# Attention, Fourier mixing and a feed-forward part on one core: other steps for three folds, and another order of ScalarE's copies and exponentials

## The chip, the cores and the metric

The kernel runs on one core of one Trainium2 chip, in one launch. The metric is the device time of one execution in microseconds (us). A core has TensorE (PE in the profile), VectorE (DVE), ScalarE (ACT), GpSimd (POOL) and a queue for data transfers (SP). Each works through its own instructions in order and waits for the others by semaphores.

## The reference

For each of 4 images (batch entries) of 768 tokens, attention with 8 heads of 64, where a token sees the first 4 tokens (the sinks) and the last 128; then a Fourier transform over tokens and over channels, of which the real part is added; then layer norm and a feed-forward part of 512 to 2048 to 512 channels.

```python
scores = scale * np.matmul(q, k.transpose(0, 1, 3, 2))
keep = is_sink | in_window
scores = np.where(keep, scores, -1000000000.0)
a = np.exp(scores - np.max(scores, axis=-1, keepdims=True))
a = a / (np.sum(a, axis=-1, keepdims=True) + 1e-09)
x = np.matmul(a, v)                       # heads side by side: (4, 768, 512)
u = x + np.real(np.fft.fft(np.fft.fft(x, axis=1), axis=2))
un = (u - mean(u)) / np.sqrt(var(u) + 1e-06)
out = u + np.maximum(un @ w_ch1, 0.0) @ w_ch2
```

## The kernel before

**Attention.** An image has 6 blocks of 128 queries, 24 in all. A block has 4 steps, one for each pair of heads, so there are 96 steps and a few more to drain. In a step each engine issues a short list of operations, most of them for a pair of some steps ago (`STEP_LAG`, `BLOCK_AT`). For a pair of heads, TensorE computes scores (L700, L702) into PSUM tiles s, of which there are two: the matmul of a pair waits until VectorE has read the pair before the last. VectorE's `merge` (L708) puts the older keys' part into place, and `soft1` (L720, twice) adds the mask and takes the negative maximum. "Pair 0" to "pair 3" below are the merges and soft1 of one block. ScalarE's `expo` (L726, two instructions) takes the exponentials and their sums. TensorE transposes the result (pt, L751), ScalarE copies it (`copy_p`: pta, L758), GpSimd masks it into ptl and pta (`newer_p`, `older_p`: L767, L775), and TensorE multiplies with the values (xt, L789). The sinks' weights go another way: GpSimd packs them (`sink_p`: sk, L737, L738), TensorE transposes them into a free part of the s tile of pair 1, two blocks later (L809), and ScalarE copies them from there (`copy_sink`: skt, L814); the merge of that pair waits for the copy. `copy_x` (xs, L794), `turn_x` (x, L801, L803) and `store_x` (L819, VectorE) bring a finished block into u, the image in token order.

**Fourier part.** When an image's fourth block is stored, `fourier` enters the steps of its transform into an event table, counted from that step. First come three folds j = 0, 1, 2, each beginning 4 steps after the one before. A fold adds and subtracts block j and block j + 3 (`fold_n`, even and odd, L351), folds the channels (`fold_m`, L358 and L361), and splits the result into a rounded part gh (`fold_hi`, ScalarE, L364) and a remainder gl (`fold_lo`, VectorE, L367). In the first three images the even half runs on VectorE and the odd half on GpSimd. The row of token 0 is handled beside that: `put_row` (L380), `mid_sum` (L371), and `mid_row`, a cast into sph (L375) and a remainder for one row (L377), both on VectorE. Seven steps after the third fold began, matmuls with cosine and sine tables read gh, gl and sph (za, zr, zb, L394; then L421, L442), VectorE forms sums (d, L447, L448), and GpSimd adds them to u (L458, L459); images 1 and 3 are then stored to DRAM by SP (ud, L461).

**Order.** Three things set it. `SCHEDULE` has, for each phase (steps before and from 36) and each of the 4 steps of a block, the list of each engine; "V", "G", "A", "T" and digits in a list are where events of the table go. `F_N`, `F_M`, `F_S` and `ROW` are the steps of the folds. From step 97 on (`CUT`) the framework orders the instructions itself, which is where the fourth image's transform (its folds wholly on VectorE) and the conversion of the feed-forward weights (cv, L590 to L592) lie. The first three images' folds lie ahead of that.

**Feed-forward part.** From about 278 us on, TensorE multiplies with resident weights (h, L619; o, L1124) to the end.

Of the kernel before, what the change touches and what calls it, by code (L numbers as in the profile page):

```python
# [25 lines left out]
NHALF = NB // 2  # L26
# [8 lines left out]
NR = 33  # L35
# [25 lines left out]
FILL_AT, FILL = (24, 36), 0  # L61
FOLD_AT, FOLD_LAST, FOLD_ENG = (0, 4, 8), (0, 4, 8), "VG"

F_N, F_M, F_S, ROW = (3, 3), (4, 5), (6, 7), (5, 8, 10)
EV_A = 0

SINK0_AT = 3, 3, "V"
# [16 lines left out]
    {  # L84
        "A": [
            ["copy_x", "copy_p", "copy_sink", "expo", "A", "sink_hi"],
            ["copy_x", "copy_sink", "expo", "sink_hi", "A", "copy_p"],
            ["copy_x", "copy_p", "copy_sink", "expo", "A", "sink_hi"],
            ["copy_x", "A", "copy_p", "copy_sink", "expo", "sink_hi"],
        ],  # L90
        "V": [
            ["inverse", "store_x", "sink_lo", "V", 3, 0, 1, 2, "merge", "soft1"],
# [17 lines left out]
    {  # L110
        "A": [
            ["copy_x", "copy_p", "A", "sink_hi", "copy_sink", "expo"],
            ["copy_x", "copy_sink", "A", "sink_hi", "copy_p", "expo"],
            ["copy_x", "copy_p", "copy_sink", "expo", "A", "sink_hi"],
            ["expo", "copy_x", "copy_p", "copy_sink", "A", "sink_hi"],
        ],
# [89 lines left out]
def kernel(  # L206
# [15 lines left out]
    V, A, G, T = nc.vector, nc.scalar, nc.gpsimd, nc.tensor  # L222

    def f32(ap):
        return ap.bitcast(F32)
# [44 lines left out]
    def run(general):  # L270
        tag = "g" if general else ""
        with ExitStack() as p1:
# [8 lines left out]
            def at(s, eng, fn):  # L281
                ev.setdefault((s, eng), []).append(fn)
# [26 lines left out]
            sph = fpool.tile([P, 384], F32R, name="sph")  # L309
# [22 lines left out]
            def fourier(b, at, ready):  # L332
# [5 lines left out]
                t_ = {}  # L338
# [9 lines left out]
                def fold_n(eng, j, odd):  # L348
                    t = fw.tile([P, DM], F32, tag=f"f{odd}", name=f"f{odd}_{b}_{j}", bufs=2 - odd)
                    t_["eo", j, odd] = t  # L350
                    eng.tensor_tensor(t, u[j], u[NHALF + j], op=ALU.subtract if odd else ALU.add)  # L351

                def fold_m(eng, j, odd):

                    g = t_["eo", j, 0]
                    if odd:
                        t = t_.pop(("eo", j, odd))
                        eng.tensor_tensor(g[:, 257:512], t[:, 1:256], t[:, 511:256:-1], op=ALU.subtract)  # L358
                        t_["g", j] = t_.pop(("eo", j, 0))
                    else:  # L360
                        eng.tensor_tensor(g[:, 1:256], g[:, 1:256], g[:, 511:256:-1], op=ALU.add)  # L361

                def fold_hi(j):
                    A.copy(gh[:, j], t_["g", j])  # L364

                def fold_lo(j):
                    V.tensor_tensor(gl[:, j], t_.pop(("g", j)), f32(gh[:, j]), op=ALU.subtract)  # L367
# [2 lines left out]
                    r = t_["x0"]  # L370
                    V.tensor_tensor(r[:, 1:256], r[:, 1:256], r[:, 511:256:-1], op=ALU.add)  # L371

                def mid_row():
                    t = t_["x0"]
                    V.tensor_copy(sph[:NR, :257], t[:, :257])  # L375
                    lo = sph[NR - 1:NR, :257]
                    V.tensor_tensor(lo, t[NR - 1:NR, :257], f32(lo), op=ALU.subtract)  # L377

# [84 lines left out]
                tail = b == B - 1 or general  # L463
                at(1, "S", load_row)
                for j in range(NHALF):
                    k = ready[j]
                    e0, e1 = FOLD_TAIL if tail else FOLD_ENG
                    eng = {"V": V, "G": G}
                    at(k + F_N[0], e0, lambda j=j: fold_n(eng[e0], j, 0))
                    at(k + F_N[1], e1, lambda j=j: fold_n(eng[e1], j, 1))  # L470
                    at(k + F_M[0], e0, lambda j=j: fold_m(eng[e0], j, 0))
                    at(k + F_M[1], e1, lambda j=j: fold_m(eng[e1], j, 1))
                    at(k + F_S[0], "A", lambda j=j: fold_hi(j))
                    at(k + F_S[1], "V", lambda j=j: fold_lo(j))
# [862 lines left out]
```

## Time and profile before

| | us |
|---|---|
| runs of the kernel | 786.68, 789.1, 787.84; median 787.84 |
| the profiled execution | 786.78 |
| its span, first to last instruction | 784.9 |
| busy: PE / DVE / ACT / POOL | 755.2 / 460.6 / 239.0 / 177.6 |

The span divides roughly so: attention with the transforms of the first three images to about 222 us, the fourth transform beside the first group of the feed-forward part to 278, the rest of the feed-forward part to the end. In rows of the profile, "L367" is line 367 of the kernel before, "gl<-f,gh" names the tile written and those read, the first number is the start, the second how long one (or a merged run of "x4") took, and square brackets tell the idle time of the engine ahead of it with what ended it. Busy times of PE include its pipelining, so a busy PE need not be at its peak.

### The profile page before, as it was taken

How to read it: one execution, taken by the hardware profiler on the slowest of the kernel's cores; microseconds unless marked ns; L12 is line 12 of the kernel's file. 1: busy time of each engine (PE TensorE's matmuls, PEld its weight loads, DVE VectorE, ACT ScalarE, POOL GpSimd, SP SyncE). 2: the span in 40 equal slices, each digit the busy share in tenths (PEclk: the TensorE clock that was granted, in tenths of full speed). 3: DMA queues.
4: the chain of work that ended last, by engine and by line, in shares of the span. 5: the costliest groups of instructions: out<-in, count | busy, mean ns of one | idle time of the engine just before them, and what ended most of it. 6: DMA issues, size and time to landing. Idle time of an engine off the chain costs nothing.

```text
span 784.9 us, 11953 instructions
## 1 busy us (share of the span) xinstructions
PE 755.2 (96%) x4379; PEld 615.8 (78%) x4379; DVE 460.6 (59%) x1354; ACT 239.0 (30%) x704; POOL 177.6 (23%) x283
## 2 busy tenths in 40 slices
PE   7999998988899999999999999999999999999996
PEld 5666876866778878899888888888888888888895
DVE  6788687999999589561356424662456425611211
ACT  4887765756633133221111111111111110110110
POOL 2566477476645255200000000000000000000000
PEclk9999999999999999999999999999999999999999
DMA  9853525433305366120100002000200001000100
GB/s 311 251 171 109 140 84 176 127 112 99 131 27 159 111 196 210 62 71 1 54 1 0 1 9 99 1 1 0 81 1 0 1 0 54 1 1 0 55 1 32
DMA packets 41812, 57.69 MB, mean 74 GB/s; under 512 B 2796, under 2 KB 27500, under 8 KB 41360
## 3 DMA queue, kind: packets, MB, share of 16 engines
q1 hardware_dynamic: 41456, 53.07, 21.7%
q0 software_dynamic: 288, 3.76, 1.2%
q8 instruction: 37, 0.61, 0.3%
q14 instruction: 31, 0.25, 0.1%
HBM read 47.37 MB, written 9.45 MB: 72 GB/s over the span
## 4 chain that ended last, share of the span: by engine, by line
PE 80%; DVE 13%; issue 2%; POOL 1%; ACT 1%; DMA 1%; SPq 0%; DVEq 0%; ACTq 0%; POOLq 0%
PE h L619 33%; PE o L1124 33%; PE xt L789 3%; PE s L702 3%; DVE sm L720 2%; PE pt L751 2%; DVE cv L591 1%; PE za L394 1%; DVE s L708 1%; DVE cv L590 1%; PE a L421 1%; DVE cv L592 1%; DVE f L351 1%; PE x L801 1%; DMA vt<-in_v_sink_dram 1%
## 5 line engine op out<-in xcount | busy, mean ns | idle before, releaser
L1124 PE MATMUL o<-w,h 128*128 128x512 f32 x876 | 216.5, 394 | 0.0
L1117 DVE SCALAR_TENSOR_TENSOR h<-h,h 128x512 fp32r<-128x512 f32 (+1 forms) x107 | 65.4, 611 | 247.7 <-ACT h L1112 247.5
L1124 PEld LDWEIGHTS o<-w,h 128*128 128x128 f32 x876 | 162.8, 188 | 35.5
L1112 ACT ACTIVATE h<-h 128x512 fp32r<-128x512 f32 (+1 forms) x107 | 57.2, 535 | 366.4 <-PE h L619 360.1
L619 PE MATMUL h<-un_slots,w 128*128 128x512 f32 (+1 forms) x576 | 124.7, 365 | 0.0
L619 PEld LDWEIGHTS h<-un_slots,w 128*128 128x128 f32 x576 | 99.6, 188 | 19.6
L619 PE MATMUL h<-un_last,w 128*128 128x512 f32 (+1 forms) x432 | 89.0, 355 | 0.0
L619 PEld LDWEIGHTS h<-un_last,w 128*128 128x128 f32 x432 | 72.7, 188 | 12.8
L726 ACT ACTIVATE sm<-sm,mx 128x132 f32<-128x132 f32 x192 | 75.8, 400 | 7.1 <-DVE mx L720 7.1
L1148 DVE STREAM_TRANSPOSE unf<-un 32x128 f32<-32x128 f32 x224 | 67.7, 302 | 3.2
L702 PE MATMUL s<-ring,q 64*128 64x260 f32 x320 | 51.2, 422 | 12.2 <-DVE mx L720 6.4
L720 DVE CUSTOM_DVE_ANT_0 sm<-s,mask 128x132 f32<-128x132 f32 x192 | 48.7, 292 | 9.3 <-ACT skt L814 2.7
L702 PEld LDWEIGHTS s<-ring,q 64*128 64x128 f32 x320 | 27.1, 188 | 28.2 <-issue 12.4
L608 POOL TENSOR_TENSOR w<-cv,w 128x512 fp32r<-128x512 f32 x25 | 33.9, 1354 | 35.5 <-ACT w L607 35.4
L789 PE MATMUL xt<-ptl,ldv 128*64 128x128 f32 x384 | 38.9, 288 | 0.0
L708 DVE COPY_PREDICATED s<-older,s 128x256 f32<-128x256 uint8 x80 | 33.6, 420 | 7.2 <-ACT skt L814 6.8
L726 ACT ACTIVATION_READ_ACCUMULATOR sm<-sm,mx 128x1 f32 x192 | 36.8, 192 | 0.0
L1124 PE MATMUL o<-w_ring,h 128*128 128x512 f32 x144 | 35.6, 393 | 0.0
L767 POOL TENSOR_SCALAR_AFFINE_SELECT ptl<-pta 128x512 f32<-128x512 f32 x48 | 32.2, 672 | 14.4 <-ACT pta L758 14.4
L789 PEld LDWEIGHTS xt<-ptl,ldv 128*64 128x64 f32 x384 | 21.6, 137 | 14.9 <-issue 8.1
L789 PE MATMUL xt<-pta,ldv 128*64 128x128 f32 x320 | 31.7, 277 | 0.2 <-POOL pta L775 0.2
L751 PE MATMUL pt<-ident,sm 128*128 128x128 f32 x192 | 31.6, 288 | 0.0
(200 smaller groups left out, 1040.9 us busy)
## 6 DMA issues: line engine op xcount, KB each, us to landing
raw<-in_moe_w_ch_dram SPq DMA_DIRECT2D x32, 512.0 KB, 3.7
ldv<-in_v_dram SPq DMA_DIRECT2D x28, 256.0 KB, 3.6
ring<-in_qk_dram SPq DMA_DIRECT2D x24, 264.0 KB, 4.6
out_dram<-u SPq DMA_DIRECT2D x24, 256.0 KB, 3.8
q<-in_qk_dram SPq DMA_DIRECT2D x20, 256.0 KB, 4.2
cst<-in_dft_dram POOLq DMA_DIRECT2D x1, 3348.0 KB, 11.7
ud<-us SPq DMA_DIRECT2D x12, 256.0 KB, 2.2
u<-ud SPq DMA_DIRECT2D x2, 1024.0 KB, 5.1
```

The costliest lines, as they stand in the source:

```text
L608: G.tensor_tensor(d[1], tf, f32(d[0]), op=ALU.subtract)
L619: T.matmul(ps[:, :tb], a[:, cs], x[:, :, cc, :], start=n == 0, stop=n == 3 * NCC - 1)
L702: T.matmul(ps[:, j, :P + W], st["q", g][rows, hp, :], keys(g, 2 * hp + j), start=True, stop=True)
L708: V.copy_predicated(ps[:, :, P + NS:P + W], older[qi > 2], ps[:, :, 0:P])
L720: V.tensor_tensor_reduce(sm[:, h % 4], ps[:, j, P:P + W], mask[min(qi, 3)], -SCALE, 3.0e38, ALU.add, ALU.min, accum_out=mx[:, 0, h:h + 1])
L726: A.activation(sm[:, h % 4], sm[:, h % 4], AF.Exp, bias=mx[:, 0, h:h + 1], scale=-1.0, accum_out=mx[:, 1, h:h + 1])
L751: T.transpose(ps[:, j], sm[:, j, NS:], ident)
L789: T.matmul(ps[D * j:D * j + D, p, :], st["v", kb(g) - i][:, h, :], a[:, h % 4, :], start=i == 0, stop=i == n - 1)
L1112: A.activation(h[0], ps[:, :tb], AF.Relu)
L1117: V.scalar_tensor_tensor(h[1], ps[:, :tb], 0.0, f32(h[0]), op0=ALU.max, op1=ALU.subtract)
L1124: T.matmul(po[i], a[:, ts_], x, start=f == 0 and n == 0, stop=f == NF - 1 and n == 2)
L1148: V.transpose(unf[32 * q:32 * q + 32, :, r], un[r].rearrange("p (c q j) -> p c q j", c=NCC, q=4)[:, :, q])
```

## The change

`F_STEPS` replaces `F_N`, `F_M`, `F_S`. For folds 0 and 1 of the first three images, the odd half's `fold_n` goes from step 3 to 4 after the fold's start, its `fold_m` from 5 to 6, gh from 6 to 7 and gl from 7 to 8. For fold 2, and in the fourth image, only the odd `fold_n` goes from 3 to 4. `mid_row` is split: its cast moves from VectorE's step 10 to ScalarE's step 9 (`mid_hi`), its remainder to step 13 (`mid_lo`). In ScalarE's lists, `expo` goes ahead of `copy_sink` in the second step of a block in both phases, where `copy_p` also goes ahead of "A" in the later phase and `sink_hi` to the end, and ahead of `copy_x`, "A" and `copy_p` in the fourth step of the earlier phase.

```diff
-F_N, F_M, F_S, ROW = (3, 3), (4, 5), (6, 7), (5, 8, 10)
+F_STEPS = ((3, 4), (4, 5), (6, 7)), ((3, 4), (4, 6), (7, 8))
+ROW = 5, 8, 9, 13
...
-            ["copy_x", "copy_sink", "expo", "sink_hi", "A", "copy_p"],
+            ["copy_x", "expo", "copy_sink", "copy_p", "A", "sink_hi"],
...
-            ["copy_x", "A", "copy_p", "copy_sink", "expo", "sink_hi"],
+            ["expo", "copy_x", "A", "copy_p", "copy_sink", "sink_hi"],
...
-            ["copy_x", "copy_sink", "A", "sink_hi", "copy_p", "expo"],
+            ["copy_x", "expo", "copy_sink", "copy_p", "A", "sink_hi"],
...
-                def mid_row():
+                def mid_hi():
+                    A.copy(sph[:NR, :257], t_["x0"][:, :257])
+
+                def mid_lo():
                     t = t_["x0"]
-                    V.tensor_copy(sph[:NR, :257], t[:, :257])
                     lo = sph[NR - 1:NR, :257]
                     V.tensor_tensor(lo, t[NR - 1:NR, :257], f32(lo), op=ALU.subtract)
...
+                    f_n, f_m, f_s = F_STEPS[0 if tail or j == NHALF - 1 else 1]
...
-                at(ready[0] + ROW[2], "V", mid_row)
+                at(ready[0] + ROW[2], "A", mid_hi)
+                at(ready[0] + ROW[3], "V", mid_lo)
```

What it does to the order is shown at three places, all in the second image's fold, first before, then after. Line numbers of the changed kernel are some lines higher (L369 is L367 before, L353 L351, L714 L708, L820 L814, L732 L726).

VectorE, from the end of pair 3 of one block to pair 2 of the next (the two soft1 behind each merge are left out):

```order
L742 TENSOR_SCALAR mx_1512<-mx_1512 128x8
L743 RECIPROCAL mx_1512<-mx_1512 128x8
L375 CAST sph<-xr_1440 33x257
L377 TENSOR_TENSOR sph<-xr_1440,sph 1x257
L367 TENSOR_TENSOR gl_1429<-f_1_1_1654,gh_1428 128x512
L351 TENSOR_TENSOR f_1_2_1778<-us_2_1072,us_5_1075 128x512
L708 COPY_PREDICATED s_0_1769<-older_122,s_0_1769 128x2x128
L708 COPY_PREDICATED s_1_1772<-older_122,s_1_1772 128x2x128
L361 TENSOR_TENSOR f_1_2_1778<-f_1_2_1778 128x255
L819 TENSOR_TENSOR u_65<-x_1805,mx_1385 128x512
L708 COPY_PREDICATED s_2_1826<-older_122,s_2_1826 128x2x128
```
```order
L748 TENSOR_SCALAR mx_1512<-mx_1512 128x8
L749 RECIPROCAL mx_1512<-mx_1512 128x8
L353 TENSOR_TENSOR f_1_2_1776<-us_2_1069,us_5_1072 128x512
L714 COPY_PREDICATED s_0_1767<-older_122,s_0_1767 128x2x128
L714 COPY_PREDICATED s_1_1770<-older_122,s_1_1770 128x2x128
L369 TENSOR_TENSOR gl_1429<-f_1_1_1653,gh_1428 128x512
L363 TENSOR_TENSOR f_1_2_1776<-f_1_2_1776 128x255
L825 TENSOR_TENSOR u_65<-x_1801,mx_1385 128x512
L381 TENSOR_TENSOR sph<-xr_1440,sph 1x257
L714 COPY_PREDICATED s_2_1825<-older_122,s_2_1825 128x2x128
```

Of the four fold instructions ahead of pair 0 one is left there; gl stands behind pair 1, the row's remainder ahead of pair 2, and the cast is gone from VectorE.

ScalarE, in the block before that one (sm_2 is a half of a block's scores with its pairs 2 and 3, sm_0 with pairs 0 and 1):

```order
L726 ACTIVATE sm_2_1584,mx_1512<-sm_2_1584,mx_1512 128x132 x2
L814 CAST skt_1690<-s_1_1645 128x128
L430 COPY asb_0_1692<-a_0_1676 128x257
L758 COPY pta_1_1694<-pt_1_1670 128x512
L726 ACTIVATE sm_2_1584,mx_1512<-sm_2_1584,mx_1512 128x132 x2
L726 ACTIVATE sm_0_1657,mx_1658<-sm_0_1657,mx_1658 128x132 x4
```
```order
L732 ACTIVATE sm_2_1584,mx_1512<-sm_2_1584,mx_1512 128x132 x4
L820 CAST skt_1689<-s_1_1644 128x128
L764 COPY pta_1_1691<-pt_1_1667 128x512
L434 COPY asb_0_1693<-a_0_1673 128x257
L732 ACTIVATE sm_0_1656,mx_1657<-sm_0_1656,mx_1657 128x132 x2
L376 CAST sph<-xr_1440 33x257
L732 ACTIVATE sm_0_1656,mx_1657<-sm_0_1656,mx_1657 128x132 x2
```

Pair 3's exponentials went ahead of the sinks' copy skt and of the copy pta, pta ahead of the transform's copy asb, and the cast into sph came in.

GpSimd, from a block's second mask to the next block's first (u_64 is image 0, to which the sums d are added; f_1_1 is the odd half of fold 1):

```order
L767 AFFINE_SELECT ptl_3_1661<-pta_3_1617 128x512
L351 TENSOR_TENSOR f_1_1_1663<-us_1_1071,us_4_1074 128x512
L458 TENSOR_TENSOR u_64<-u_64,d_2_1580 128x257
L459 TENSOR_TENSOR u_64<-u_64,d_2_1580 128x255
L737 CAST sk_1627<-sm_2_1584 128x2x16
L738 TENSOR_TENSOR sk_1627<-sm_2_1584,sk_1627 128x2x16
```
```order
L773 AFFINE_SELECT ptl_3_1660<-pta_3_1616 128x512
L462 TENSOR_TENSOR u_64<-u_64,d_2_1580 128x257
L463 TENSOR_TENSOR u_64<-u_64,d_2_1580 128x255
L353 TENSOR_TENSOR f_1_1_1704<-us_1_1068,us_4_1071 128x512
L743 CAST sk_1625<-sm_2_1584 128x2x16
L744 TENSOR_TENSOR sk_1625<-sm_2_1584,sk_1625 128x2x16
```

The fold's first instruction stands behind the update of u instead of ahead of it. On TensorE the order up to the framework's part is the same.

More of the change, by code (lines that the diff above doesn't have):

```diff
@@ L466, in fourier @@
                     k = ready[j]
+                    f_n, f_m, f_s = F_STEPS[0 if tail or j == NHALF - 1 else 1]
                     e0, e1 = FOLD_TAIL if tail else FOLD_ENG
                     eng = {"V": V, "G": G}
[L469 to L474, printed above, removed]
+                    at(k + f_n[0], e0, lambda j=j: fold_n(eng[e0], j, 0))
+                    at(k + f_n[1], e1, lambda j=j: fold_n(eng[e1], j, 1))
+                    at(k + f_m[0], e0, lambda j=j: fold_m(eng[e0], j, 0))
+                    at(k + f_m[1], e1, lambda j=j: fold_m(eng[e1], j, 1))
+                    at(k + f_s[0], "A", lambda j=j: fold_hi(j))
+                    at(k + f_s[1], "V", lambda j=j: fold_lo(j))
                 at(ready[0] + ROW[0], "V", put_row)
                 at(ready[0] + ROW[1], "V", mid_sum)
-                at(ready[0] + ROW[2], "V", mid_row)
+                at(ready[0] + ROW[2], "A", mid_hi)
+                at(ready[0] + ROW[3], "V", mid_lo)
                 k = ready[2] + S1
```

## The prediction, made before the changed kernel was run

> **What bounds the kernel now.** First the busy times by stretch, to see which engine each stage runs out of. Columns: stretch and its length, busy time of PE, weight load, DVE, ACT and POOL with their instruction counts, granted clock, DMA share, GB/s.
>
> ```profile
> 98.00:131.00 33.00, 29.01 (x243) 22.42 (x239) 27.93 (x97) 20.93 (x79) 23.64 (x40) 0.95 0.35 111
> 131.00:160.00 29.00, 28.62 (x262) 22.98 (x258) 25.88 (x114) 19.04 (x72) 15.05 (x33) 1.00 0.49 138
> 160.00:190.00 30.00, 24.08 (x200) 18.23 (x200) 29.14 (x91) 18.32 (x67) 21.73 (x35) 1.00 0.39 124
> 278.00:785.00 507.00, 499.74 (x2362) 414.51 (x2361) 226.67 (x548) 78.07 (x142) 22.75 (x18) 1.00 0.10 35
> ```
>
> From 278 us on TensorE is busy 499.74 of 507 us with the feed-forward part, which the change does not touch: what is won before 278 us is kept. Between two folds (131 to 160) TensorE is full too, 28.62 of 29. In the second image's fold (98 to 131) it lacks 3.99 us and in the third's (160 to 190) 5.92 us, and there VectorE is the full engine, 29.14 of 30 in the third. So the change can win only in the fold stretches. Next, what TensorE waited for in 98 to 131 (total, times, longest):
>
> ```profile
> PE s L702 <- DVE mx L720: 2.7, 3, 2.3
> PE s L702 <- DVE d L448: 1.2, 1, 1.2
> ```
>
> One hole of 2.3 us stands out: score matmuls that wait for VectorE's soft1. The other, 1.2 us at 106.7, ends when a key load issued at 103.0 can have landed; the change does not move that load, so I cost it at 0 (it would be -1.2 if it went). The hole in TensorE's timeline, and the granted clock behind it:
>
> ```profile
> 117.40 0.47 PE L803 MATMUL x<-vs,skt 128*128 128x512 f32 x1
> 120.19 0.71 PE L702 MATMUL s<-ring,q 64*128 64x260 f32 x4 [2.31 <-DVE mx L720]
> 124.90 1.15 PE L702 MATMUL s<-ring,q 64*128 64x260 f32 x8
> ```
> ```profile
> 120.00:122.00 2.00, 1.62 (x10) 0.69 (x10) 1.97 (x10) 1.64 (x8) 1.92 (x5) 0.85 0.00 0
> 122.00:124.00 2.00, 2.00 (x18) 1.67 (x18) 1.79 (x12) 0.00 (x0) 1.85 (x5) 0.50 0.00 0
> 124.00:126.00 2.00, 2.00 (x14) 1.30 (x14) 0.62 (x2) 1.57 (x3) 1.77 (x4) 0.79 0.43 138
> ```
>
> TensorE was ready at 117.9 and started at 120.19; then its clock was 0.85, 0.50 and 0.79 of full for 2 us each, another 2 x (0.15 + 0.50 + 0.21) = 1.7 us. That place costs 4.0 us in all. Its cause is a burst on VectorE:
>
> ```profile
> 106.52 1.51 DVE L367 TENSOR_TENSOR gl<-f,gh 128x512 fp32r<-128x512 f32 x1
> 107.96 1.12 DVE L351 TENSOR_TENSOR f<-us,us 128x512 f32<-128x512 f32 x1
> 109.00 0.41 DVE L708 COPY_PREDICATED s<-older,s 128x256 f32<-128x256 uint8 x1
> 109.89 0.42 DVE L708 COPY_PREDICATED s<-older,s 128x256 f32<-128x256 uint8 x1
> 115.00 0.65 DVE L375 CAST sph<-xr 33x257 fp32r<-33x257 f32 x1
> 115.69 0.74 DVE L377 TENSOR_TENSOR sph<-xr,sph 1x257 fp32r<-1x257 f32 x1
> 116.46 1.01 DVE L367 TENSOR_TENSOR gl<-f,gh 128x512 fp32r<-128x512 f32 x1
> 117.39 1.76 DVE L351 TENSOR_TENSOR f<-us,us 128x512 f32<-128x512 f32 x1
> 119.07 0.41 DVE L708 COPY_PREDICATED s<-older,s 128x256 f32<-128x256 uint8 x1
> 121.19 0.69 DVE L819 TENSOR_TENSOR u<-x,mx 128x512 f32<-128x512 f32 x1
> ```
>
> Four fold instructions (L375, L377, L367, L351) take 115.00 to 119.07, 4.07 us, ahead of the first pair's merge. A pair (merge and two soft1) takes 0.89 us, 109.00 to 109.89.
>
> **The change part by part.** Times are those of the trace of before; each step tells where its instruction would stand.
>
> *Second image.* In the first of its two fold blocks, L367 (106.52) goes behind pair 1; pair 0 is then done by 108.5 at the latest. Pair 1 cannot follow at once, because its merge waits for ScalarE's skt copy:
>
> ```profile
> 109.17 0.27 ACT L814 CAST skt<-s 128x128 fp32r<-128x128 f32 x1 [2.06 <-PE s L809]
> L814 ACT CAST skt<-s x22: 245/267/268, 20.0 to 196.8; 128x128 fp32r<-128x128 f32 x22
>   PE s L809: 24.4, 18
> ```
>
> TensorE's transposition stays where it was, so VectorE idles to 109.4, ends pair 1 at 110.3, and has L367 still to do. How long that takes is open:
>
> ```profile
> 55.18 0.69 DVE L367 TENSOR_TENSOR gl<-f,gh 128x512 fp32r<-128x512 f32 x1
> 116.90 1.70 POOL L351 TENSOR_TENSOR f<-us,us 128x512 f32<-128x512 f32 x1
> ```
>
> The same instruction takes 0.6 start to start at 55.18 and 1.44 at 106.52; L351 took 1.68 at 117.39, beside POOL's own L351 at 116.90. I take 0.9, between, as POOL is busy 23.64 of 33 us here; ends 0.6 and 1.44. VectorE reaches L361 at 111.2 instead of 110.78 (109.89 and a pair's 0.89), and everything to 115.00 is 0.4 later.
>
> A page bears on this. The Trainium skill (GPSIMD Engine Reference, 1. Specifications) says that GpSimd shares its SBUF interfaces with VectorE and contends with VectorE instructions that have two SBUF inputs. That speaks against the change: a fold instruction that is moved takes its contention along, and by it alone the moved L367 keeps its 1.44 and 0.93 us. The trace agrees, 0.69 against 1.51 us; by the page's rule the sum below would be about 1 us smaller.
>
> In the second fold block the burst at 115.4 is L351 alone (0.6 to 1.68; I take 1.1, nearer the row beside POOL): 116.5. Pair 0 ends 117.4 instead of 119.96, before TensorE is ready at 118.3 (117.9 and the 0.4): the hole is gone. Pair 1, held by skt, ends 118.9; L367 0.9, L361 0.35, store_x 0.6 and L377 0.4 to 0.77 follow, 121.3; pair 2 ends 122.2, and the score matmuls of 124.90 start at 122.4. Their second half waits for pair 3. I take **-2.2** (ends -3.8, hole and clock whole, and -1.2, all contended).
>
> *Third image.* Here VectorE sets the pace throughout, so moving work saves nothing; leaving it out does.
>
> ```profile
> 171.98 0.56 DVE L375 CAST sph<-xr 33x257 fp32r<-33x257 f32 x1
> 172.57 1.37 DVE L377 TENSOR_TENSOR sph<-xr,sph 1x257 fp32r<-1x257 f32 x1
> 175.39 0.27 ACT L814 CAST skt<-s 128x128 fp32r<-128x128 f32 x1 [1.92 <-PE s L809]
> ```
>
> L375 goes (0.59 start to start), L377 may shrink from 1.37 towards the second image's 0.74; but with 2.0 us of L375 and L377 and 1.0 of L367 taken from ahead of pair 0, pair 0 ends about 174.5 and pair 1 waits for skt to 175.6 (175.39 and the copy), a new wait of 1.1. Net **-0.6** (-1.6 to +0.5).
>
> *First image.*
>
> ```profile
> 62.21 0.23 DVE L375 CAST sph<-xr 33x257 fp32r<-33x257 f32 x1
> 64.53 0.27 ACT L814 CAST skt<-s 128x128 fp32r<-128x128 f32 x1 [0.96 <-PE s L809]
> ```
>
> L375 goes here too, 0.23, and L367 leaves the place ahead of pair 0. Pair 0 would then end about 63.9, and pair 1 waits for skt to 64.8, 0.9, with L367 still behind it: what is won ahead of the wait is lost in it. The other fold block of this image is of the same kind. **0** (-0.5 to +0.5).
>
> *Fourth image* (scheduled by the framework):
>
> ```profile
> 226.24 0.72 DVE L375 CAST sph<-xr 33x257 fp32r<-33x257 f32 x1
> ```
>
> 0.65 less on VectorE, which is nearly full there; half of it counts, as TensorE is the fuller engine by then: **-0.3** (-0.65 to +0.5).
>
> *ScalarE.* The copies to sph (four, bounded by L814's 0.27 and the 0.65 above) lie in its idle time, 12 of 33 us in 98 to 131. An exponential pair (0.8 us) now goes ahead of skt. Behind the waiting skt stood that pair, the copy pta, and with them POOL:
>
> ```profile
> POOL sk L737 <- ACT sm L726: 58.7, 30, 8.8
> ```
>
> skt waits 24.4 us in 18 cases, 1.36 on average, so the pair fits: 0. If it did not, pair 1's merge would be later by up to 0.8. In the fold blocks quoted here the wait was 0.96, 1.92 and 2.06; before step 36, where it is shorter, another pair leaves the place ahead of skt in exchange. POOL gets its input sooner by the wait and by the copies that stood between; TensorE's waits in 98 to 131 name VectorE alone, so I count 0.
>
> *POOL and SP.* L351 and L358 go behind L775 and the u updates; gh, which waits for L358, has until its old time. The update stores move with them, and on SP one passes a weight load:
>
> ```profile
> 184.79 0.33 SPq L581 DMA_DIRECT2D raw<-in_moe_w_ch_dram  x1
> 185.97 0.32 SPq L461 DMA_DIRECT2D ud<-us  x1
> raw<-in_moe_w_ch_dram SPq DMA_DIRECT2D x32, 512.0 KB, 3.7
> ```
>
> The load is issued some 1.5 us later and lands about 190, over 10 us before its conversion is due (after 201): 0.
>
> Sum: -2.2 - 0.6 + 0 - 0.3 = -3.1. The profiled execution took 786.78 us (span 784.9 and 1.9 around it), so 783.7; the median of the runs shown, 787.84, is 1.06 above it, which gives **784.7**.
>
> **Rivals.** *Moved, not removed.* VectorE has the same work in the folds, contention included, and the hole only goes to the place behind pair 1. For it: the third image's 29.14 of 30. Against it: in the second image TensorE's hole is one piece, with slack around it. Then the copies to sph alone leave: 0.27 + 0.69 + 0.59 = 1.55, time 786.3.
>
> *A new hole, slower.* In the third image, behind pair 1, un (L538), L367, L361, the row's sum, store_x and pair 2 now follow each other.
>
> ```profile
> 167.03 0.90 DVE L538 TENSOR_SCALAR un<-u,stat 128x512 f32<-128x512 f32 x1
> ```
>
> If all are contended that is 0.9 + 1.44 + 0.8 + 0.4 + 0.7 + 0.9 = 5.1 us after pair 1's 0.9, 6.0 against some 4 us of TensorE's own work (its 24.08 us of 30 over the three blocks there, halved between the two pairs): 2 us of waiting. From the size of the hole that lowered the clock (2.31) on it costs 1.7 more. With the second image's hole kept behind pair 1 as well, that is about +3: 790.8.
>
> *More than said.* Later there is a second such place:
>
> ```profile
> 209.57 0.62 PE L394 MATMUL zb<-cst,gh 128*128 128x386 f32 x2 [2.05 <-DVE zb L409]
> ```
> ```profile
> 210.00:212.00 2.00, 2.00 (x10) 1.90 (x9) 2.00 (x7) 0.62 (x1) 0.65 (x2) 0.54 0.17 20
> ```
>
> If conversions meet less POOL work after a shift of 3 us, and this wait falls under what lowers the clock, 2 to 3 us more go: 781.8. The Trainium skill (TensorE: Matmul & The Clock Gate, HAM oscillation) names idle gaps of over about 3.4 us as what throttles; by it a wait of 2.05 would cost no clock, and this rival would give 783.5. The trace speaks otherwise: behind 2.31 us it was 0.50, behind 2.05 us 0.54.
>
> **How the numbers follow.** The forecast has 0.50, moved-not-removed 0.27, more than said 0.13, the new hole 0.10. The forecast's own range is -5 to -1.3, 782.8 to 786.5; the range given reaches down to most of the third rival and up past the first: **781.0 to 788.3**, leaving the new hole and a tail below. About 0.3% (2.4 us) is what a measurement tells from no change, so faster is under 785.5: 0.40 of the forecast's 0.50 and the 0.13, together **0.53**; same 0.10 + 0.27 = **0.37**; slower **0.10**.
>
> **What would show it.** In the changed kernel's profile the second image's longest wait of TensorE for soft1 is under 1 us, and the clock stays at 1.00 through its fold; VectorE waits for skt in the fold blocks, once about 1 us in each image; the time from 160 to 190 shrinks by less than 1 us; nothing changes from the feed-forward part on but its start. I am wrong if TensorE shows a wait of 2 us or more in any fold, if L367 takes 1.4 us at its new place, or if skt comes later than its transposition in blocks where it waited before.

## The result: 792.85 us after 787.84, and where it arose

| | before | after |
|---|---|---|
| median of five runs each, us | 787.84 | 792.85 |
| profiled execution, us | 786.78 | 792.28 |
| its span, us | 784.9 | 790.5 |

The ratio of the runs is 1.0075, 95% interval 1.006 to 1.0091: 5 to 6 us slower where 3 us faster was forecast. In these texts a ratio is turned into us by 787.

A block's last matmul (x, L803 before, L809 after) gives a clock that both traces have. Its start, in us:

```
block            2      5      6      7     11     12     13     16     19     23   span
before       39.11  57.19  64.69  73.02 110.22 117.40 128.84 155.52 187.73 220.96  784.9
after        39.98  57.89  67.43  76.70 113.91 121.75 131.52 158.66 193.34 226.34  790.5
later by      0.87   0.70   2.74   3.68   3.69   4.35   2.68   3.14   5.61   5.38    5.6
```

The plain blocks lose 0.9, the first image's fold (blocks 5 to 7) 3.0, the stretch from 13 to 16 0.5 and the third's fold (16 to 19) 2.5; the second's (11 to 13) gains 1.0; from block 19 on nothing changes. The busy times of the changed kernel by stretches, columns as before (TensorE, its weight loads, VectorE, ScalarE, GpSimd, granted clock, DMA share, GB/s):

```profile
50.00:76.00 26.00, 22.57 (x195) 15.43 (x195) 21.36 (x86) 18.49 (x72) 17.88 (x32) 0.93 0.41 120
98.00:131.00 33.00, 28.70 (x262) 22.16 (x259) 26.59 (x101) 21.64 (x81) 24.57 (x42) 1.00 0.35 105
131.00:160.00 29.00, 28.56 (x249) 23.15 (x250) 26.30 (x111) 19.00 (x71) 14.75 (x30) 1.00 0.49 151
160.00:190.00 30.00, 23.95 (x201) 17.77 (x203) 27.44 (x97) 18.13 (x66) 23.32 (x36) 0.93 0.35 107
278.00:785.00 507.00, 505.25 (x2386) 418.79 (x2384) 232.10 (x559) 79.30 (x144) 24.67 (x20) 1.00 0.11 36
```

The second image's clock went from 0.95 to 1.00, as forecast, and VectorE is busy 26.59 us there instead of 27.93. But two new rows with 0.93 stand in the first and third images. TensorE's timeline (start, duration, idle time before) has their holes and what became of the second image's 2.31:

```profile
62.61 2.18 PE L708 MATMUL s<-ring,q 64*128 64x260 f32 x8 [1.67 <-issue]
118.23 0.71 PE L708 MATMUL s<-ring,q 64*128 64x260 f32 x4 [0.76 <-PE pt L757]
127.08 0.71 PE L708 MATMUL s<-ring,q 64*128 64x260 f32 x4 [1.46 <-issue]
185.66 1.13 PE L708 MATMUL s<-ring,q 64*128 64x260 f32 x4 [1.93 <-issue]
```

All four are score matmuls that start 0.1 us after a soft1 of VectorE's has ended, whatever releaser the row names ("issue" only says that the inference found none). The granted clock behind the first and the last, in slices of 2 us (the clock is the third number from the end):

```profile
62.00:64.00 2.00, 1.39 (x6) 0.82 (x8) 1.93 (x12) 1.62 (x5) 1.61 (x4) 0.74 0.74 185
64.00:66.00 2.00, 2.00 (x16) 1.34 (x16) 1.52 (x6) 1.75 (x9) 1.93 (x3) 0.50 0.02 4
66.00:68.00 2.00, 2.00 (x20) 1.52 (x18) 0.43 (x1) 0.73 (x3) 0.80 (x3) 0.91 0.00 0
...
186.00:188.00 2.00, 1.34 (x6) 0.58 (x5) 2.00 (x8) 1.15 (x6) 2.00 (x3) 0.50 0.28 108
188.00:190.00 2.00, 2.00 (x18) 1.39 (x16) 1.97 (x8) 0.00 (x0) 1.37 (x3) 0.50 0.29 109
190.00:192.00 2.00, 2.00 (x13) 1.67 (x10) 0.23 (x4) 0.23 (x2) 0.00 (x0) 0.50 0.95 268
192.00:194.00 2.00, 2.00 (x12) 1.92 (x11) 1.55 (x7) 1.31 (x6) 1.33 (x2) 0.84 0.05 20
```

Lost to the clock: 2 x (0.26 + 0.50 + 0.09) = 1.7 us in the first image and 2 x (3 x 0.50 + 0.16) = 3.3 in the third, against 1.7 regained in the second. That is 3.3 us net, set against 5.6 lost in all, and an upper bound on the clock's part: the third image's fold lost only 2.5 us, less than its 3.3 at half clock, so some of these lie where TensorE would have waited anyway. The rest is the holes themselves and the plain blocks.

One sum of waits changed much as well. VectorE's wait for the sinks' copy (total, times, longest), first in the changed kernel, then before:

```profile
DVE s L714 <- ACT skt L820: 13.4, 15, 1.9
```
```profile
DVE s L708 <- ACT skt L814: 6.8, 11, 1.3
```

### The profile page after: what moved, and what is told of

Same layout as the page of the kernel before. It is cut to its first block, busy times and chain, and to the rows that moved or that the text cites. A ratio compares the mean times of both kernels' runs of the same rounds, so it can differ in the third digit from the quotient of the medians.

```text
span 790.5 us, 11966 instructions
## 1 busy us (share of the span) xinstructions
PE 757.8 (96%) x4379; PEld 617.9 (78%) x4379; DVE 459.1 (58%) x1350; ACT 240.5 (30%) x708; POOL 179.4 (23%) x283
## 4 chain that ended last, share of the span: by engine, by line
PE 76%; DVE 14%; DMA 3%; issue 2%; ACT 2%; SPq 1%; POOL 1%; DVEq 0%; ACTq 0%; POOLq 0%
PE o L1130 32%; PE h L625 32%; PE xt L795 3%; PE s L708 3%; DMA ring<-in_qk_dram 2%; DVE cv L597 2%; DVE sm L726 2%; PE pt L757 1%; DMA ldv<-in_v_dram 1%; PE za L398 1%; DVE s L714 1%; ACT sm L732 1%; DVE cv L596 1%; DVE cv L598 1%; DVE gl L369 1%
## 5 line engine op out<-in xcount | busy, mean ns | idle before, releaser
L732 ACT ACTIVATE sm<-sm,mx 128x132 f32<-128x132 f32 x192 | 75.6, 398 | 7.4 <-DVE mx L726 7.4
L708 PE MATMUL s<-ring,q 64*128 64x260 f32 x320 | 52.3, 431 | 14.3 <-issue 6.3
L726 DVE CUSTOM_DVE_ANT_0 sm<-s,mask 128x132 f32<-128x132 f32 x192 | 48.7, 292 | 9.6 <-ACT skt L820 2.8
L708 PEld LDWEIGHTS s<-ring,q 64*128 64x128 f32 x320 | 27.8, 192 | 29.8 <-issue 16.4
L714 DVE COPY_PREDICATED s<-older,s 128x256 f32<-128x256 uint8 x80 | 33.7, 421 | 14.3 <-ACT skt L820 13.4
L732 ACT ACTIVATION_READ_ACCUMULATOR sm<-sm,mx 128x1 f32 x192 | 36.6, 190 | 0.0
```

The source lines that it names most:

```text
L708: T.matmul(ps[:, j, :P + W], st["q", g][rows, hp, :], keys(g, 2 * hp + j), start=True, stop=True)
L714: V.copy_predicated(ps[:, :, P + NS:P + W], older[qi > 2], ps[:, :, 0:P])
L726: V.tensor_tensor_reduce(sm[:, h % 4], ps[:, j, P:P + W], mask[min(qi, 3)], -SCALE, 3.0e38, ALU.add, ALU.min, accum_out=mx[:, 0, h:h + 1])
L732: A.activation(sm[:, h % 4], sm[:, h % 4], AF.Exp, bias=mx[:, 0, h:h + 1], scale=-1.0, accum_out=mx[:, 1, h:h + 1])
```

## The experiments

The first theory (A) came from this: gl and the row's remainder left the place ahead of the wait for skt, where they had cost nothing, and now stand behind it, ahead of the next scores. Rival B: ScalarE's lists make skt late. Rival C: the row's split, since ScalarE now waits for the row's sum. Each run is compared with runs of the kernel before beside it, whose medians were 786.7 to 787.4.

**e1 to e4: which part.** The change has three: lists, fold steps, row. e1, e2, e3 each have one alone (the other two as before); e4 has lists and row, with the steps undone:

```diff
-F_STEPS = ((3, 4), (4, 5), (6, 7)), ((3, 4), (4, 6), (7, 8))
+F_STEPS = ((3, 3), (4, 5), (6, 7)), ((3, 3), (4, 5), (6, 7))
```

> The kernel before with the new lists of ScalarE alone (fold steps and the row's steps as before). Theory A (the loss is made by the moved fold and row steps: they left the place ahead of VectorE's wait for skt, so VectorE idles there, 13.4 us instead of 6.8, and comes late to the next merges, which leaves TensorE holes of 1.67 and 1.93 us with half clock behind each): this kernel has neither hole, keeps the second image's hole of 2.31 with its half clock, and takes 787.0 to 789.0. Theory B (the lists make skt late): VectorE's waits for skt are near 13 us already here and the time is above 790.

> The kernel before with the new fold steps alone (lists and row as before). Theory A: the first image's hole of about 1.67 us at the last block of its fold is there with half clock behind it, worth +2 to +3; the second image's hole is shorter than 2.31; the third image's hole, without the row's 0.83 in it, stays under 1.3 us; together 787.5 to 790. Theory B: 784 to 787, since only the second image's gain is left. A third, C (the row's difference at its new place and the copies to sph that wait for the row's sum on ScalarE): as B here.

> The kernel before with the row's split alone (copy to sph on ScalarE a step earlier, the difference three steps later; lists and fold steps as before). Theory A: no hole in the first image; the second image's hole of 2.31 is shortened or gone, since 0.27 to 0.69 leave the place ahead of it; the third image's longer by 0.83 but not beyond 1.9; 784.5 to 788. Theory C: above 789.5, with ScalarE waiting 5 us for the row's sum and its exponentials late behind it.

> The changed kernel with the fold steps put back as they were (new lists and the row's split stay). Theory A: the first image's hole is gone, the third image's hole under 1.6 us and with full clock, VectorE's waits for skt down from 13.4 to under 10 us; 785 to 788.5. Theories B and C: the loss stays, above 790.

| run | median, us | ratio, interval | us by the ratio |
|---|---|---|---|
| e1 lists | 791.05 | 1.0061, 1.0047 to 1.0074 | +4.8 |
| e2 steps | 786.01 | 0.9992, 0.9980 to 1.0004 | -0.6 |
| e3 row | 784.83 | 0.9979, 0.9966 to 0.9991 | -1.7 |
| e4 lists and row | 790.66 | 1.0057, 1.0044 to 1.0070 | +4.5 |

e1 and e4 lie above A's ranges and e2 below its; e3 lies within A's, but the moved fold work alone, in e2, loses nothing, and that was A's point. C falls in e3. So the moved fold work is not the loss, the lists are. The mechanism named in B does not hold for e1, though: VectorE's wait for skt was 6.7 us there, as before.

What differs in e1's trace is where GpSimd waits. In the kernel before it mostly stands ahead of its packing operation sk, waiting for exponentials (58.7 us, the row in the prediction). With the lists this wait is half as long, and its wait ahead of the masks, for the copy pta, is longer. The rows are first e1's, then that of the kernel before (a line's number differs by a few from kernel to kernel):

```profile
POOL sk L740 <- ACT sm L729: 29.0, 24, 5.6
POOL ptl L770 <- ACT pta L761: 39.0, 32, 2.5
```
```profile
POOL ptl L767 <- ACT pta L758: 14.4, 12, 2.5
```

The two waits together are 68.0 us instead of 73.1, so on the whole GpSimd is hardly freed; what changes is the moment at which its masks and its half of the fold run, and they then meet VectorE's fold operations at other places. From this, theory D: the two engines' operations on SBUF wait for each other, and GpSimd used to be out of VectorE's way because it was late.

**e5, e6: the two lists before step 36 apart.** Each exchanges one list in the kernel before:

```diff
-            ["copy_x", "copy_sink", "expo", "sink_hi", "A", "copy_p"],
+            ["copy_x", "expo", "copy_sink", "copy_p", "A", "sink_hi"],
...
-            ["copy_x", "A", "copy_p", "copy_sink", "expo", "sink_hi"],
+            ["expo", "copy_x", "A", "copy_p", "copy_sink", "sink_hi"],
```

> The kernel before with only ScalarE's list of the second place in a block (k = 1, the steps before 36) exchanged: exponentials ahead of the copy of the sinks, copy of the values ahead of the rest. Of the 3.8 us that all lists cost, 0.85 arose in the plain block ending at 40, 0.6, 0.7 and 1.1 in the three blocks of the first image, and none behind step 36. Theory D (the lists let POOL begin its selects and its half of the fold earlier, just as VectorE begins its own fold operations on the same operands in the chip's memory, and the two then wait for each other: L353 on VectorE took 1.76 beside POOL's 1.71, against 0.69 in the kernel before): the list that frees POOL sooner carries the loss, wherever skt falls. Theory B (skt late behind the pair of exponentials): this list, which alone puts exponentials ahead of skt, carries all of it, 790 to 792, and VectorE's waits for skt grow. By D VectorE's waits for skt stay near 6.8 us, and this list alone costs 0.8 to 2 (the plain block's share), 787.5 to 789.5.

> The kernel before with only ScalarE's list of the fourth place in a block (k = 3, the steps before 36) exchanged: the exponentials first. Theory D: POOL gets its exponentials sooner and no longer stands waiting while VectorE folds; VectorE's fold operations in 50 to 72 are longer by 1.5 us or more, and the time is 788.5 to 790.5. Theory B: nothing changes for skt, so 786.5 to 788.

e5: 789.45, ratio 1.0039 (1.0025 to 1.0053), +3.1, with VectorE's waits for skt at 7.7; e6: 789.26, 1.0036 (1.0022 to 1.0051), +2.8. Both times lie in D's ranges, e5 at the upper end; B has no account of e6, since the sinks' copy has no work in the fourth place of a block. VectorE's fold operations from 50 to 72 us are 1.1 us longer in e6, where D had named 1.5. The collision in e6, in the first image (VectorE, GpSimd, TensorE):

```profile
64.04 1.20 DVE L377 CAST sph<-xr 33x257 fp32r<-33x257 f32 x1
65.28 0.73 DVE L379 TENSOR_TENSOR sph<-xr,sph 1x257 fp32r<-1x257 f32 x1
```
```profile
63.83 1.27 POOL L353 TENSOR_TENSOR f<-u 128x512 f32<-128x512 f32 x1
65.05 0.69 POOL L778 TENSOR_SCALAR_AFFINE_SELECT pta<-pta 128x512 f32<-128x512 f32 x1
```
```profile
68.38 0.71 PE L705 MATMUL s<-ring,q 64*128 64x260 f32 x4 [1.63 <-DVE mx L723]
```

The cast began 0.21 us after GpSimd's L353 and ended 0.14 us after it; it had taken 0.23 in the kernel before (the row at 62.21 in the prediction), where GpSimd waited for exponentials until 62.86. TensorE's wait at this place was 0.15 us then.

**e7, e8: the change without lists, and with the one behind step 36 alone.** e7 is the changed kernel with all three lists as before, e8 with the two before step 36 as before.

> The changed kernel with all lists of ScalarE put back: fold steps and the row's split alone. By the sums of the single runs (-0.6 and -1.6 against 787.2 measured beside them) 784 to 786; by a theory in which steps and row hurt each other in the third image (1.93 us of hole and 6 us at half clock in the changed kernel, where the steps alone had 1.03 and the row alone 0.88) 787 to 789.

> The changed kernel with only the two lists before step 36 put back; the list behind step 36 stays new. Theory D, by which the loss of the lists lies wholly before step 36: the same as fold steps and row alone within 1 us, 784 to 786.5, and the second image as good as in the changed kernel. Theory B: the remaining list still makes skt late behind step 36, 787 to 789.

e7: 787.20, ratio 0.9999 (0.9985 to 1.0013). e8: 792.60, 1.0078 (1.0063 to 1.0093), +6.1. Steps and row together gain nothing, though the row alone gained 1.7. And the list behind step 36 costs 6 us beside them: missed by both theories as worded. (No run has that list alone in the kernel before.)

**e9, e10, e13, e14: inside that list.** From ["copy_x", "copy_sink", "A", "sink_hi", "copy_p", "expo"], the old list, e13 moves only "expo", to the place ahead of "copy_sink"; e14 moves only "copy_p", to the place behind it (both on e7). e9 is e8, and e10 the changed kernel, with skt first again:

```diff
-            ["copy_x", "expo", "copy_sink", "copy_p", "A", "sink_hi"],
+            ["copy_x", "copy_sink", "expo", "copy_p", "A", "sink_hi"],
```

> As e8, but in the list behind step 36 the copy of the sinks stands ahead of the exponentials again (the early copy of the values stays). In e8, skt came at 66.80, behind two pairs of exponentials, where it came at 66.58 behind one in e7 and its transposition was done by 65.7; VectorE then waited 1.99 for it. Theory B (skt comes late by the pair that was put ahead of it, 0.8 us each time, and TensorE's next scores with it): VectorE's waits for skt fall back by 3 us or more and the time returns to that of e7, 786 to 788.5. Theory D (POOL's earlier start alone): the time stays at 791 to 793.

> The changed kernel with the copy of the sinks ahead of the exponentials again in both lists that had put it behind; all else as changed. Theory B: 788 to 790, since what is left is the list of the fourth place in a block (2.2 by e6) and the early copy of the values. Theory D: 791.5 to 793.5.

> As e7 (fold steps and row), and in ScalarE's list behind step 36, second place, only the exponentials moved, from the end to ahead of skt; the copy of the values stays at the end. Of the 5.4 us between e7 (787.2) and e8 (792.6), e9 gave back 2.4 by putting skt ahead again. Theory B (skt late by a pair): 789.5 to 792.6, VectorE's waits for skt near 13.9 as in e8 against 11.5 in e7. Theory F (the early copy of the values is what costs, since it lets POOL's selects begin while VectorE folds, and since the transform's copies come behind it): 786.5 to 788.5.

> As e7, and in ScalarE's list behind step 36, second place, only the copy of the values moved ahead of the transform's copies; the exponentials stay last and skt stays second. Theory F: 789 to 792. Theory B: 786.5 to 788.5.

e13: 791.43, ratio 1.0049 (1.0033 to 1.0064), 3.9 us above e7, with VectorE's waits for skt at 13.5. e14: 787.06, 0.9997 (0.9983 to 1.0011), nothing. So the early exponentials carry it. e9: 790.23, 1.0036 (1.0024 to 1.0048), 3.3 less than e8 and between the ranges of B and D. e10: 791.98, 1.0070 (1.0051 to 1.0089), not told apart from the changed kernel. With that the order of skt and exponentials is a part of the loss and not all of it. e9 does not tell B from D, though: VectorE's waits for skt fell only from 13.9 to 13.0 us, not by the 3 that B had named, and GpSimd's wait for exponentials rose from 50.9 to 60.6, as skt put first also holds the exponentials back. Single places of the traces show two mechanisms side by side. First, skt behind another pair of exponentials, in the first image, in e7 and then in e8 (TensorE's transposition, ScalarE's copy, VectorE's merge, TensorE's next scores):

```profile
65.90 0.31 PE L815 MATMUL s<-ident_r,sk 128*128 128x128 f32 x1
66.58 0.25 ACT L820 CAST skt<-s 128x128 fp32r<-128x128 f32 x1
66.86 0.43 DVE L714 COPY_PREDICATED s<-older,s 128x256 f32<-128x256 uint8 x1 [1.22 <-ACT skt L820]
67.99 0.71 PE L708 MATMUL s<-ring,q 64*128 64x260 f32 x4 [0.47 <-DVE mx L726]
```
```profile
65.35 0.31 PE L815 MATMUL s<-ident_r,sk 128*128 128x128 f32 x1
66.80 0.25 ACT L820 CAST skt<-s 128x128 fp32r<-128x128 f32 x1
67.08 0.43 DVE L714 COPY_PREDICATED s<-older,s 128x256 f32<-128x256 uint8 x1 [1.99 <-ACT skt L820]
68.21 0.71 PE L708 MATMUL s<-ring,q 64*128 64x260 f32 x4 [1.24 <-DVE mx L726]
```

The copy came 0.68 us after the transposition's start in e7 and 1.45 in e8, VectorE waited 0.77 longer, and TensorE 0.77 longer: one pair of exponentials, handed through. Second, the collision, in the third image, in e7 and then in e13. Up to pair 1 the two agree, and VectorE waits 1.05 us for skt in both; what differs is that in e7 GpSimd has to wait for exponentials.

```profile
180.12 0.25 POOL L743 CAST sk<-sm 128x32 fp32r<-128x32 f32 x1 [0.88 <-ACT sm L732]
179.61 0.69 DVE L369 TENSOR_TENSOR gl<-f,gh 128x512 fp32r<-128x512 f32 x1
180.21 0.43 DVE L363 TENSOR_TENSOR f<-f 128x255 f32<-128x255 f32 x1
181.28 0.42 DVE L381 TENSOR_TENSOR sph<-xr,sph 1x257 fp32r<-1x257 f32 x1
182.73 0.45 DVE L596 TENSOR_SCALAR cv<-raw 128x512 int32<-128x512 int32 x1
183.70 0.71 PE L708 MATMUL s<-ring,q 64*128 64x260 f32 x4 [0.75 <-PE pt L757]
```
```profile
180.52 0.21 POOL L743 CAST sk<-sm 128x32 fp32r<-128x32 f32 x1
180.96 0.74 DVE L369 TENSOR_TENSOR gl<-f,gh 128x512 fp32r<-128x512 f32 x1
181.62 0.85 DVE L363 TENSOR_TENSOR f<-f 128x255 f32<-128x255 f32 x1
183.10 0.84 DVE L381 TENSOR_TENSOR sph<-xr,sph 1x257 fp32r<-1x257 f32 x1
184.97 0.93 DVE L596 TENSOR_SCALAR cv<-raw 128x512 int32<-128x512 int32 x1
181.11 1.09 POOL L773 TENSOR_SCALAR_AFFINE_SELECT ptl<-pta 128x512 f32<-128x512 f32 x1
182.93 0.73 POOL L360 TENSOR_TENSOR f<-f 128x255 f32<-128x255 f32 x1
184.90 0.73 POOL L463 TENSOR_TENSOR us<-us,d 128x255 f32<-128x255 f32 x1
186.43 0.71 PE L708 MATMUL s<-ring,q 64*128 64x260 f32 x4 [2.13 <-issue]
```

The four operations of VectorE take 0.05 + 0.42 + 0.42 + 0.48 = 1.37 us more, and TensorE's hole is 2.13 - 0.75 = 1.38 longer. Nothing else is needed to explain this hole: the three long ones began inside the three rows of GpSimd and ended 0.27 or 0.28 us after them. The place is 1.4 of the 3.4 us by which e13's span is longer than e7's (789.2 and 785.8). The largest other share is in the first image's last fold block, 3.0 us with two holes of 1.23 and 1.28 and a stretch at half clock, of which the second image gives 2.3 back, where e7 has its own half clock.

Added up over 26 to 196 us the traces say the same, with a warning. As an estimate, take what each VectorE operation beside one of GpSimd's took beyond the same operation with none beside it (the median of all traces here). It comes to 14.9 us in the kernel before and 17.0 in e1; to 9.5 in e7, 11.9 in e13 and 12.0 in e8, and there GpSimd's masks make most of the increase (4.2, 6.4, 6.4) and its fold little (3.1, 3.6, 3.7). The warning is that the changed kernel, the slower one, has 12.4 against the 14.9 before: the place of a collision counts, ahead of scores for which TensorE waits, and not the sum.

**e11, e12, e15: without GpSimd's half of the fold.** In the first three transforms the odd half is left out, so these kernels do not compute the transform: in the kernel before (e11), in e6 (e12) and in e1 (e15):

```diff
                 def fold_n(eng, j, odd):
+                    if odd and not tail:
+                        return
...
-                    if odd:
+                    if odd and not tail:
+                        t_["g", j] = t_.pop(("eo", j, 0))
+                    elif odd:
                         t = t_.pop(("eo", j, odd))
```

> The kernel before without POOL's half of the fold in the first three transforms (both of its operations for each half are left out, so the odd halves are not subtracted). It is the base for e12. VectorE's fold operations that began inside POOL's took up to 1.76 instead of 0.69, together 7.8 us longer than alone from 26 to 196 in the kernel before, about half of it beside POOL's fold. By theory D VectorE's fold operations are mostly at 0.69 and 0.42 here, the second image's hole of 2.31 (behind an L351 of 1.76) is under 1.4 with no half clock, and the time is 783 to 785.5; if POOL's fold costs VectorE nothing that counts, 786.5 to 788.

> e6 (only the list of the fourth place in a block) without POOL's half of the fold in the first three transforms. Theory D (that list's 2.2 us is POOL's fold coming early, on top of VectorE's fold operations): within 0.7 us of e11. If the list costs by ScalarE's order itself, 2 us or more above e11.

> e1 (the new lists alone) without POOL's half of the fold in the first three transforms, to be compared with e11 (784.1, the same without the lists). With POOL's fold the lists cost 4.8 us (e1 less the 787.2 or so measured beside it would be 3.8; by the ratio 1.0061 it is 4.8). Theory D (collision of POOL's fold with VectorE's): within 1.5 us of e11. Theory B (skt late, whatever POOL does): 3 us or more above e11.

e11: 784.12, ratio 0.9961 (0.9946 to 0.9976), so GpSimd's fold costs the kernel before 3.1 us; but the second image's hole stayed, at 2.09, against the expectation. e12: 785.74, 0.9985 (0.9974 to 0.9996), 1.9 above e11, where the list had cost 2.8 with the fold. e15: 786.81, 0.9987 (0.9974 to 1.0000), 2.0 above e11, where the lists had cost 4.8. Both lie between their expectations, e12 near the one against D. Without GpSimd's fold the fourth list thus keeps two thirds of its loss, and all lists together lose less than half of theirs; each figure is a difference of two ratios that are known to about 1 us each. Its masks, which stayed, are a part of the rest: in e15 block 2, ahead of every fold, takes 0.85 us longer than before, as in e1. How much of the rest they are was not separated.

**e16, e17: can it be better than both?** e16 is e3 with the odd sums one step later; e17 is e3 with the opposite of the change's order, in the fourth list behind step 36:

```diff
-F_STEPS = ((3, 3), (4, 5), (6, 7)), ((3, 3), (4, 5), (6, 7))
+F_STEPS = ((3, 4), (4, 5), (6, 7)), ((3, 4), (4, 5), (6, 7))
```
```diff
-            ["expo", "copy_x", "copy_p", "copy_sink", "A", "sink_hi"],
+            ["copy_x", "A", "copy_p", "copy_sink", "expo", "sink_hi"],
```

> The best kernel so far, e3 (the row's split alone, 784.8), with POOL's odd sum one step later in all halves, and VectorE's low halves at their old steps. If the spreading of POOL's operations away from VectorE's is what the fold steps gain, and VectorE's low halves behind the second pair are what they lose, 783 to 784.8; if the two parts hurt each other whatever is spread, 785.5 to 787.5, as e7.

> e3 (the row's split alone, 784.8) with the opposite of the change's idea in ScalarE's list of the fourth place behind step 36: the exponentials last but one instead of first, as the kernel before has them ahead of step 36. If it is POOL's early start that costs (theory D), and ScalarE has time to spare, holding the exponentials back costs nothing and keeps POOL away from VectorE's fold operations a little longer: 783 to 785.5. If later exponentials make TensorE wait for them (pt), 787 or more.

e16: 785.74, ratio 0.9982 (0.9969 to 0.9994), not told apart from e3; its median lies in the second of its two ranges. e17: 789.76, 1.0038 (1.0025 to 1.0051): worse, and not by pt, as its expectation had it. GpSimd's waits for exponentials are 77.2 us there, and now TensorE waits for GpSimd's masks:

```profile
PE xt L795 <- POOL pta L781: 1.4, 1, 1.4
PE xt L795 <- POOL ptl L773: 1.4, 1, 1.4
```

Collisions are fewest there, 6.8 us by the estimate above, and it is slower than e3 (13.1) all the same. That fits the reading that GpSimd's lateness is free only inside a band, in which the kernel before stood; no run shows where the band ends. The version that beats both kernels is e3, the row's split alone: 784.83, 0.9979, with e16 beside it.

## Why the prediction was wrong, by its own steps

- **ScalarE: the step that failed.** It was put at 0: "skt waits 24.4 us in 18 cases, 1.36 on average, so the pair fits", and, for GpSimd's earlier input, "TensorE's waits in 98 to 131 name VectorE alone, so I count 0". Measured, the lists cost 4.8 us alone and 6 beside steps and row. The first half of the step went by an average: in the block at 66 us of e8 there was no slack, as ScalarE came late from a cast (gh) that the change had put a step later and that had waited for GpSimd, and the price named for that case, up to 0.8, is what it cost, 0.77. The second half asked whether an earlier input helps, and not what an engine whose work falls at other moments will run into: 1.37 us of collisions at the place in e13's third image. How the 6 us divide between the two is open.
- **Second image, -2.2: the second step that failed.** The hole that was named did go, 2.31 became 0.76. But the burst had moved and not gone: 1.46 us arose at 127.08, behind pair 1, where the moved gl met GpSimd's fold (122.77 to 124.05):

```profile
123.08 1.51 DVE L369 TENSOR_TENSOR gl<-f,gh 128x512 fp32r<-128x512 f32 x1
```

  I had taken 0.9 for it, between ends of 0.6 and 1.44. The change moves gl of fold 1 and GpSimd's `fold_n` of fold 2 by one step each, so that both stand in step 11 before and in step 12 after it: the objection that a moved instruction takes its contention along was right. The lists are not the cause, since e7, without them, has it worse (VectorE, GpSimd, TensorE), with half clock behind the hole:

```profile
121.66 1.83 DVE L369 TENSOR_TENSOR gl<-f,gh 128x512 fp32r<-128x512 f32 x1
121.67 1.27 POOL L353 TENSOR_TENSOR f<-us,us 128x512 f32<-128x512 f32 x1
125.99 0.71 PE L708 MATMUL s<-ring,q 64*128 64x260 f32 x4 [1.78 <-issue]
```

  There blocks 11 to 13 take 19.29 us, against 18.62 before. That the changed kernel has 1.00 as its clock, and 1.0 us left of the gain, is luck as far as these traces show. e3, with gl in its old place, has the whole gain, 2.0 us between blocks 11 and 13 (16.60 us): the row's split alone brings it.
- **Third image, -0.6.** +2.5: a hole of 1.93 and half clock behind it. In e7, without the lists, the same place has 0.75, and blocks 16 to 19 take 30.12 us, 2.1 less than before: without the lists the sign was right and the size too small.
- **First image, 0.** +3.0 in the changed kernel, again a hole (1.67) with half clock; +0.6 in e7. Its gl took 1.09 behind pair 1 in place of 0.69.
- **Plain attention, 0.** +0.9 in the changed kernel, as in e1, e4 and e15, which share the new second list before step 36; there two small VectorE operations of 0.21 and 0.26 met GpSimd's masks and took 0.63 and 0.69. e5, with that list alone, took 0.38 and 0.69. In e10, with skt ahead of the exponentials, they keep 0.21 and 0.26, and this loss is not there.
- **Fourth image, -0.3.** From block 23 to the end 563.94 us before, 564.16 after: nothing.
- **Rivals.** The one called "a new hole, slower" (790.8) was the nearest, in its place (third image, behind pair 1), its kind (contended operations) and its size (2 us of hole and the clock). It lay outside the range because I took the fold's own spreading as its only cause; by e7 that is not enough, so its price came near for a cause that it did not name. "Moved, not removed" holds for steps and row together: e7 is 787.2. Its trace has 5.4 us fewer collisions than the kernel before, and VectorE's waits for skt are 4.7 us longer (11.5 and 6.8): most of the time freed ahead of that wait was spent in it.
- **What was to show it.** The second image's mark came (0.76, clock 1.00). Of the signs of being wrong, L367 took 1.51 at its new place, and skt waited for its transposition 15 times instead of 18, so that in at least three blocks it came later. No hole reached the 2 us named; 1.67 and 1.93 lowered the clock all the same.

## What to carry to other kernels

An engine's wait may be what keeps it out of another's way: before removing or moving such a wait, list what the engine will start then, and which operations of the critical engine share its memory path at that moment. An average wait says nothing of the one block where it is zero; the slack to look up is that of the block that sets the pace. Try the parts of a change one by one: here the least of three gained 1.7 us, and the one that was thought harmless lost 5.

## What the hardware showed besides

**Collision.** An addition, cast, copy or TENSOR_SCALAR of VectorE with all operands in SBUF that begins inside one of GpSimd's instructions ends, in all but a few cases, about 0.1 us less than its own time after GpSimd's has ended. The cast of 0.23 above ended 0.14 us after, the operations of 0.42 in e13 0.27 or 0.28, and the L351 at 117.39 in the prediction (0.69 alone) 0.55. Not every operation on SBUF is hit: the reciprocal kept 0.20 inside GpSimd's instructions and the batch-norm statistics their 0.66 within some 5%. Merges and soft1, which read scores in PSUM, kept their 0.43 and 0.29 in every trace from 20 us on. The Trainium skill (GPSIMD Engine Reference, 1. Specifications) says that GpSimd shares its SBUF interfaces with VectorE, with contention for VectorE instructions in a 2-port perf mode or with two SBUF inputs. The traces agree for two inputs (gl, 0.69 alone and 1.51 in the changed kernel); the cast has one input, and no run here shows in which mode it ran. That VectorE waits until GpSimd's instruction is over is what these rows show.

**Clock.** Stretches at half clock last 3.4 us (1.7 us lost each) or twice that, and the size of a hole alone does not decide: 1.67 us brought one in the changed kernel, while 2.13 in e13 brought none, nor did anything in e3, whose clock is 1.00 from 26 us to the end of the folds, over the same 2.06 us of waiting for zb that lowered it in the other two. The rows of e13 behind 186.43, then those of e3:

```profile
186.00:188.00 2.00, 0.71 (x4) 0.33 (x4) 2.00 (x11) 0.99 (x5) 1.93 (x3) 1.00 0.55 208
188.00:190.00 2.00, 1.78 (x21) 1.30 (x22) 2.00 (x7) 0.78 (x4) 1.92 (x4) 1.00 0.00 0
```
```profile
160.00:200.00 40.00, 35.88 (x309) 28.51 (x310) 36.61 (x123) 26.06 (x94) 29.45 (x48) 1.00 0.39 121
200.00:235.00 35.00, 29.77 (x213) 25.41 (x212) 34.95 (x66) 14.66 (x35) 22.00 (x21) 1.00 0.19 61
```

In each trace the stretches begin a whole number of 3.41 us apart: in the changed kernel at 62.94 and 185.82 (36 times), in the kernel before at 121.41 and 210.16 (26 times), as the slices above and in the prediction also give. The Trainium skill (TensorE: Matmul & The Clock Gate, Part 1) says that activity is judged in free-running windows of 3.4 us. The length of the stretches and the spacing of their starts agree, and it would then be a matter of where a hole falls in a window; how much idle time in one is enough, no run here settles.

One stretch more or less is worth up to 1.7 us, so it can hide or treble a step worth 1 us. Runs of one kernel scatter, the longer ones mostly with the lower clock: e7 took 784.76 to 789.55 us, with a mean clock of 0.996 in the shortest run and 0.989 in the longest.
